# Batch one of an attention-and-mixer kernel read two steps per partition in all three pairs of chunks

## The chip, the core and the metric

The kernel runs on one core of a Trainium2 chip. A core has five engines with a queue of instructions each: TensorE (PE; weight loads, which overlap products, are shown apart as PEld), VectorE (DVE), ScalarE (ACT), GpSimd (POOL) and SyncE (SP), which here only issues DMAs. Sixteen DMA engines move the data. The metric is device time in microseconds (us), lower is better. Before the change it was 164.72 us, the median of 3 runs (164.44 to 165.76).

## The reference

The first half is a linear attention with a decaying state, for 4 batches, 8 heads, 768 steps and 48 values per head; the second half is an MLP mixer over its output (768 steps by 384 columns per batch).

```
for t in range(S):                                       # S = 768
    cur = einsum('bhd,bhe->bhde', u[None] * k[:, :, t], v[:, :, t])
    y[:, :, t] = einsum('bhd,bhde->bhe', r[:, :, t], state + cur)
    state = w[None, :, :, None] * state + einsum('bhd,bhe->bhde', k[:, :, t], v[:, :, t])

xt = x.transpose(0, 2, 1)                                # x: batch, 768, 384
h = maximum(xt @ w_tok1, 0) @ w_tok2                     # 768 -> 256 -> 768
u = x + h.transpose(0, 2, 1)
out = u + maximum(u @ w_ch1, 0) @ w_ch2                  # 384 -> 1536 -> 384
```

## The kernel before

**Attention in chunks.** Each batch's 768 steps are cut into six chunks of 128. For a chunk, k and r are multiplied by powers of the decay (tables `wnat`, `wp`, `wpair`; the products are called `kr`), turned on PE or by a DMA transpose, and multiplied with each other (`at_ps`); DVE masks the result to the earlier steps (`AT`). y is AT by v plus r by the state before the chunk (`S`). The state is kept in one bank for two or three chunks (`kv_ps`). The term of a step with itself goes apart: u-weighted sums of r by k (`pr`, `ad_ps`, `adg`), times v (`yd`, `ydb`), are added to y. The result of a chunk is `x_b`.

**Three ways of reading.** The list `STYLES` has one entry per chunk. "dma" (batches three and four): k, r and v of a chunk are loaded with one step per partition, so each piece of a load is 48 numbers, 192 bytes, and the turning is done by DMA. "f32" (chunks three to six of batch one, all of batch two): k and v as before, but r of a pair of chunks is loaded with two consecutive steps per partition, in pieces of 384 bytes (`window`, tile `win`); PE turns. "win" (the first pair of batch one): k, r and v are all loaded so, into one buffer of the pool `zr`, which later holds the mixer's hidden values; `pair_unit` computes the pair. In it each of the two halves j (even and odd steps) of a partition's row is scaled, turned and scored for itself, and the two chunks z of the pair lie in the upper and lower 64 partitions. So a product over one chunk's steps runs on 64 rows, twice, in place of once on 128.

**The mixer** of a batch follows: hidden products over steps (`h_ps<-x_b,wtok`, tasks `hid`), the transposed way back (`hx_ps`, `hT_ps`), up products (`z_ps<-uT,wch`), relu into `zr`, down products (`h_ps<-wch,zr`), output sums (`osb`) and stores. PE works on the up and down products of one batch while the others prepare the attention of the next.

**The order.** All work is entered as tasks; `ORDER` is a list of task numbers that says in which order they are written, and with that the order on every engine's queue. `BUFS` gives the buffer of each pool for each use, `ENGINES` the choice where a task can run on either of two engines, and `POOLS` the number of buffers. Nothing is reordered when the kernel runs: an engine whose next instruction waits holds up all behind it, and SP's queue so holds loads, DMA transposes and stores in one row. Sixteen tasks of products on a zero tile (`warm`) stand in PE's first 13 us. `GROUPS` says which chunks are scored together, `H1_PARTS` in which pieces the hidden products run, `PE_ADDS` for which chunks PE adds the own term.

**Names in the profile.** A line of nearly all rows is 279, that of the helper which records instructions, so rows are told apart by tiles. In `pair_unit` the turned k is `tk_ps` and its copy `ka`, the turned r `tr_ps` and its copy `rkb`; outside it they are `trk`, `rka`.

## Time and profile before

| | before |
|---|---|
| median of 3 runs | 164.72 us |
| the profiled execution | 164.68 us |
| its span, first to last instruction | 163.0 us |
| busy of the span: PE, DVE, ACT, POOL | 95%, 74%, 43%, 46% |
| moved by DMA | 26.90 MB in 90982 packets, 85714 of them under 512 B |
| first up product of batch one (z) | 32.9 us |
| last of PE's products ends | 159.4 us |

The profile is of one execution. The page gives busy time, the span in 40 slices of 4.07 us with a digit for tenths of a slice, the chain of waits that ended last, and groups of instructions. Other views give the instructions of an engine in order of time, busy time by stretches, and what one tile's instructions wait for. In rows of the order in time, the first number is the start and the second how long the group took, both in us; the brackets at the end name what the engine waited for ahead of it. Ends of products on PE are modelled, so the time that a group takes is best read from its start to the start of the next.

### The profile page before, as it was taken

Reading aid. Unit: us, or ns where it says so; the run is one execution under the profiler, and the core shown is the slowest. Engines: PE = TensorE matmul, PEld = TensorE weight load, DVE = VectorE, ACT = ScalarE, POOL = GpSimd, SP = SyncE. Lnnn points to the kernel's source line nnn. Section 1 sums busy time; section 2 is a strip of 40 time slices with the busy share of each in tenths; the row PEclk is TensorE's granted clock in tenths of the full one; section 3 lists DMA queues with packets and bytes.
Section 4 is the critical chain, followed back from the end, with each engine's and each line's share of the span. In section 5 each row is a group of like instructions: output and inputs, shape, how many; then the busy total and the mean of one; then the engine's idle time right before and its main releaser. Section 6 shows DMA issues by size and latency. Waiting matters only on the chain.

```text
span 163.0 us, 3866 instructions
## 1 busy us (share of the span) xinstructions
PE 154.6 (95%) x1513; PEld 104.6 (64%) x1513; DVE 120.2 (74%) x238; ACT 70.4 (43%) x162; POOL 75.2 (46%) x97
## 2 busy tenths in 40 slices
PE   6999399999999999899999999999999999999991
PEld 2457267677676768566666776777667666666670
DVE  6629997645699979998979989899598257741522
ACT  3948376586862577335262523056532101410400
POOL 7366657276007169798917947745824000000000
PEclk9999959999999999999999999999999999999999
DMA  4999999999996989999998997999971052530142
GB/s 124 262 220 190 210 211 206 196 216 192 218 200 134 191 152 182 194 195 201 189 179 172 223 221 131 201 245 180 196 189 49 2 117 67 136 120 0 48 147 99
DMA packets 90982, 26.90 MB, mean 165 GB/s; under 512 B 85714, under 2 KB 90068, under 8 KB 90964
## 3 DMA queue, kind: packets, MB, share of 16 engines
q1 hardware_dynamic: 88608, 23.40, 72.8%
q0 software_dynamic: 2160, 3.15, 11.4%
q8 instruction: 12, 0.20, 0.5%
q10 hardware_dynamic: 196, 0.11, 0.2%
q14 instruction: 6, 0.05, 0.1%
HBM read 20.46 MB, written 4.72 MB: 154 GB/s over the span
## 4 chain that ended last, share of the span: by engine, by line
PE 81%; DVE 8%; POOL 4%; issue 2%; DMA 2%; ACT 0%; DVEq 0%; ACTq 0%
PE z_ps L279 29%; PE h_ps L279 28%; PE y_ps L279 5%; PE kv_ps L279 5%; PE at_ps L279 3%; PE hT_ps L279 3%; PE hx_ps L279 2%; DVE kr L279 2%; POOL yd L279 2%; DMA out_dram<-osb 2%; DVE AT L279 2%; PE tr_ps L279 1%; PE trk L279 1%; DVE osb L279 1%; PE w_ps L279 1%
## 5 line engine op out<-in xcount | busy, mean ns | idle before, releaser
L279 PE MATMUL h_ps<-wch,zr 128*128 128x384 bf16 (+1 forms) x300 | 54.2, 320 | 0.0
L279 PE MATMUL z_ps<-uT,wch 128*128 128x384 bf16 x288 | 51.5, 326 | 0.0
L279 ACT ACTIVATE zr<-z_ps 128x384 bf16<-128x384 f32 x60 | 27.5, 490 | 45.0 <-PE z_ps L279 44.9
L279 PEld LDWEIGHTS <-wch 128*128 128x128 bf16 x288 | 31.6, 114 | 13.2
L279 PEld LDWEIGHTS <-zr 128*128 128x128 bf16 x300 | 27.5, 98 | 15.4
L279 DVE TENSOR_TENSOR AT<-at_ps,mask 128x512 bf16<-128x512 f32 x44 | 28.3, 683 | 1.2 <-PE at_ps L279 1.0
L279 DVE TENSOR_SCALAR zr<-z_ps 128x384 bf16<-128x384 f32 x36 | 19.2, 552 | 12.7 <-PE z_ps L279 12.4
L279 POOL TENSOR_TENSOR kr<-kt,wnat 128x384 bf16<-128x384 f32 x16 | 16.5, 1038 | 4.9 <-DMA kt<-in_k_dram 4.1
L279 POOL TENSOR_TENSOR yd<-vb,adg 128x384 f32<-128x384 bf16 x16 | 13.8, 866 | 6.3 <-DVE adg L279 6.1
L279 PEld LDWEIGHTS <-kr 128*128 128x128 bf16 (+1 forms) x184 | 12.0, 101 | 5.9 <-issue 2.1
L279 DVE TENSOR_TENSOR osb<-u_sb,h_ps 128x384 f32<-128x384 bf16 (+1 forms) x16 | 8.1, 524 | 6.3 <-PE h_ps L279 3.7
L279 POOL TENSOR_TENSOR ku<-kt,u_bc 128x384 f32<-128x384 f32 x10 | 9.9, 999 | 3.1 <-DMA kt<-in_k_dram 3.1
L279 DVE TENSOR_TENSOR x_b<-y_ps,yd 128x384 bf16<-128x384 f32 x18 | 9.5, 552 | 2.5 <-PE y_ps L279 1.6
L279 POOL TENSOR_TENSOR pr<-rka,rkb 128x512 bf16<-128x512 bf16 x3 | 3.6, 1210 | 15.3 <-DVE rkb L279 9.9
L279 ACT CAST vb<-vt 128x384 bf16<-128x384 f32 x19 | 9.6, 514 | 2.1 <-POOL yd L279 1.0
L279 PEld LDWEIGHTS <-wtok 128*128 128x128 bf16 x78 | 7.4, 98 | 4.6 <-issue 0.2
L279 DVE TENSOR_TENSOR u_sb<-x_b,hT_ps 128x384 bf16<-128x384 bf16 x15 | 7.7, 549 | 2.8 <-PE hT_ps L279 2.6
L279 ACT CAST S<-kv_ps 48x192 bf16<-48x192 f32 x24 | 7.5, 311 | 5.1 <-PE kv_ps L279 4.6
L279 POOL TENSOR_TENSOR rku<-ku,rt 128x384 f32<-128x384 f32 x7 | 7.2, 1031 | 4.3 <-DVE ku L279 4.2
L279 PE MATMUL y_ps<-vb,AT 128*128 128x48 bf16 (+1 forms) x208 | 8.9, 184 | 0.0
L279 PE MATMUL h_ps<-x_b,wtok 128*128 128x384 bf16 x48 | 8.8, 326 | 0.0
L279 PE MATMUL kv_ps<-warm 128*128 128x512 bf16 (+1 forms) x25 | 6.7, 425 | 1.3 <-DVE warm L279 1.3
(108 smaller groups left out, 201.6 us busy)
## 6 DMA issues: line engine op xcount, KB each, us to landing
out_dram<-osb SPq DMA_DIRECT2D x23, 192.0 KB, 2.3
kt<-in_k_dram SPq DMA_DIRECT2D x22, 192.0 KB, 5.3
vt<-in_v_dram SPq DMA_DIRECT2D x22, 192.0 KB, 4.3
rt<-in_r_dram SPq DMA_DIRECT2D x12, 192.0 KB, 3.6
win<-in_r_dram SPq DMA_DIRECT2D x5, 384.0 KB, 6.1
wch<-in_moe_w_ch_dram POOLq DMA_DIRECT2D x4, 384.0 KB, 6.7
wtok<-in_moe_w_tok_dram POOLq DMA_DIRECT2D x2, 384.0 KB, 6.2
wch<-in_moe_w_ch_dram POOLq DMA_DIRECT2D x1, 768.0 KB, 11.3
```

What stands on the lines that cost most here:

```text
L279: return lambda *args, **kw: tc.keep_in_program_order(f(*args, **kw))
```

## The change

All three pairs of batch one are now computed by `pair_unit`: `STYLES` has six "win" entries in place of two. The three rooms for their loads are three buffers of `zr`. The decay tables of k (`wk`), which lay in one of those buffers, go into two buffers of `u_sb`, and the two masks for pairs (`mask`, now bf16, and `spots`) share a third; `u_sb` is otherwise first wanted by a later half batch. The pools `ka`, `adg2` and `vb2` get a second buffer, `ydb` has three in place of four, `ku` two in place of three. `ORDER`, `BUFS` and `ENGINES` are new from end to end. The core of the diff, with a line or two of each table:

```diff
 ORDER = [
-    0, 3, 24, 54, 56, 1, 11, 895, 47, 55, 4, 2, 9, 900, 23, 6, 16, 59, 8, 13, 22, 888, 40, 7, 19, 25, 17, 12,
+    0, 3, 21, 18, 16, 56, 60, 13, 17, 59, 2, 879, 8, 5, 20, 57, 62, 872, 14, 6, 1, 42, 4, 27, 7, 11, 23, 9,
...
     'ydb': [
-    0, 1, 2, 3, 0, 1,
+    0, 1, 2, 0, 1, 0,
...
-GROUPS = [[(0, 1), (2,), (3,), (4,), (5,)], [(0, 1), (2, 3), (4, 5)], [(0, 1), (2, 3), (4, 5)],
+GROUPS = [[(0, 1), (2, 3), (4, 5)], [(0, 1), (2, 3), (4, 5)], [(0, 1), (2, 3), (4, 5)],
  [(0, 1), (2, 3), (4, 5)]]
-STYLES = 2 * [('win', 'pe')] + 10 * [('f32', 'pe')] + 12 * [('dma', 'dve')]
+STYLES = 6 * [('win', 'pe')] + 6 * [('f32', 'pe')] + 12 * [('dma', 'dve')]
...
-H1_PARTS = [[(0, 1, 2), (3, 4), (5,)], [(0, 1, 2, 3, 4, 5)], [(0, 1, 2, 3, 4, 5)], [(0, 1, 2, 3, 4, 5)]]
+H1_PARTS = [[(0, 1), (2, 3), (4, 5)], [(0, 1, 2, 3, 4, 5)], [(0, 1, 2, 3, 4, 5)], [(0, 1, 2, 3, 4, 5)]]
...
-POOLS = {'win': 3, 'ka': 1, 'rkb': 2, 'pr2': 1, 'adg2': 1, 'vb2': 1, 'ydb': 4, 'AT0': 3, 'AT1': 3}
+POOLS = {'win': 3, 'ka': 2, 'rkb': 2, 'pr2': 1, 'adg2': 2, 'vb2': 2, 'ydb': 3, 'AT0': 3, 'AT1': 3, 'ku': 2}
...
-    def early_room():
-        t = sb("zr", [128, 3, dm * 2], f32)
-        early["wk"] = t[:, 0, :].rearrange("p (j d) -> p j d", j=2)
-        early["mask"] = t[:, 1, 0:2 * T].rearrange("p (j t) -> p j t", j=2)
+    def early_wk(j):
+        def f():
+            early["wk", j] = sb("u_sb", [128, 3 * dm // 2], f32)[:, 0:dm]
+        return f
+
+    def early_masks():
+        t = sb("u_sb", [128, 3 * dm], bf16)
+        early["mask"], early["spots"] = (t[:, i * 2 * T:(i + 1) * 2 * T].rearrange("p (j t) -> p j t", j=2) for i in range(2))
...
     def two_steps(b, c, i):
-        return STYLE[b * C + c][0] == "win" or i == 1 and wide(b)
+        return STYLE[b * C][0] == "win" or i == 1 and wide(b)
...
     for b in range(B):
-        for c in range(0, C, 2):
-            if STYLE[b * C + c][0] == "win":
+        if STYLE[b * C][0] == "win":
+            for c in range(0, C, 2):
                 rooms[b, c] = room(b, c)
...
-            if STYLE[b * C + cs[0]][0] == "win":
+            if STYLE[b * C][0] == "win":
                 pair_unit(b, cs[0] // 2)
```

How this moves instructions shows on three engines. First DVE, from the copy of the first pair's turned k (`ka`) on; `AT` are the masks, `pr` the products of r and k, `S` a state, `win`, `kt` and `zr` the loads. Before:

```order
L279 COPY ka<-tk_ps 128x1024
L279 MEMSET S_1_95 128x192
L279 MEMSET S_0_94 128x192
L279 TENSOR_TENSOR pr_259<-tr_ps,ka 128x1024
L279 TENSOR_TENSOR AT_282<-at_ps,zr 128x512
L279 TENSOR_TENSOR AT_297<-at_ps,zr 128x512
L279 TENSOR_TENSOR AT_313<-at_ps,zr 128x512
L279 TENSOR_TENSOR AT_330<-at_ps,zr 128x512
L279 TENSOR_TENSOR kr_72<-win,wpair 128x8x48
L279 TENSOR_TENSOR kr_67<-kt,wnat_82 128x8x48
L279 TENSOR_TENSOR kr_72<-win,wpair 128x8x48
L279 TENSOR_TENSOR pr<-trk,rkb 128x512
```

With the change:

```order
L279 COPY ka<-tk_ps 128x1024
L279 TENSOR_TENSOR pr_252<-tr_ps,ka 128x1024
L279 TENSOR_TENSOR kr_71<-zr,u_sb 128x8x48
L279 TENSOR_TENSOR AT_310<-at_ps,u_sb 128x512
L279 TENSOR_TENSOR pr_324<-tr_ps,ka 128x1024
L279 TENSOR_TENSOR AT_331<-at_ps,u_sb 128x512
L279 TENSOR_TENSOR AT_364<-at_ps,u_sb 128x512
L279 TENSOR_TENSOR AT_377<-at_ps,u_sb 128x512
L279 TENSOR_TENSOR AT_409<-at_ps,u_sb 128x512
L279 TENSOR_TENSOR S_454<-kv_ps,wGm_91 128x384
L279 TENSOR_TENSOR AT_469<-at_ps,u_sb 128x512
L279 TENSOR_TENSOR pr_481<-tr_ps,ka 128x1024
```

The three scale products behind the first four masks are gone from this place; most of the second and third pairs' scale products now stand ahead of the copy of `ka`, and the masks of the pairs follow each other with the pairs' `pr` between them.

SP's first loads, in pieces of 96 numbers (two steps) or 48 (one). Before:

```order
L279 DMA zr<-in_r_dram 128x8x96
L279 DMA zr<-in_k_dram 128x8x96
L279 DMA win<-in_r_dram 128x8x96
L279 DMA zr<-in_v_dram 128x8x96
L279 DMA kt<-in_k_dram 128x8x48 x2
L279 DMA win<-in_r_dram 128x8x96
L279 DMA kt<-in_k_dram 128x8x48
L279 DMA vt<-in_v_dram 128x8x48
```

With the change:

```order
L279 DMA zr<-in_r_dram 128x8x96
L279 DMA zr<-in_k_dram 128x8x96 x2
L279 DMA zr<-in_r_dram 128x8x96
L279 DMA zr<-in_v_dram 128x8x96
L279 DMA zr<-in_k_dram 128x8x96
L279 DMA zr<-in_r_dram 128x8x96
L279 DMA zr<-in_v_dram 128x8x96
L279 DMA win<-in_r_dram 128x8x96
L279 DMA zr<-in_v_dram 128x8x96
```

Eight loads of k and v of 192 KB became four of 384 KB, the third pair's v stands tenth, and r of batch two (`win`) ahead of it.

POOL's queue from the first mixer weights (`wtok`) to the up weights (`wch`); `ydb` are the own terms. Before:

```order
L279 DMA wtok_98<-in_moe_w_tok_dram 128x6x256
L279 TENSOR_TENSOR ydb<-vb_234,adg_389 128x384 x2
L279 TENSOR_TENSOR kr_69<-kt,wnat_82 128x8x48
L279 TENSOR_TENSOR ydb<-vb,adg 128x384 x2
L279 DMA wtok_99<-in_moe_w_tok_dram 128x1536
L279 DMA wch_0_100<-in_moe_w_ch_dram 128x3x512
L279 DMA wch_1_101<-in_moe_w_ch_dram 128x3x1024
L279 TENSOR_TENSOR ydb<-vb,adg 128x384 x2
```

With the change:

```order
L279 DMA wtok_97<-in_moe_w_tok_dram 128x6x256
L279 TENSOR_TENSOR kr_71<-zr,u_sb 128x8x48
L279 TENSOR_TENSOR kr_72<-zr,wpair 128x8x48 x2
L279 TENSOR_TENSOR ydb<-vb_240,adg_333 128x384 x2
L279 TENSOR_TENSOR ydb<-vb_389,adg_387 128x384 x2
L279 TENSOR_TENSOR kr_67<-win,wpair 128x8x48
L279 DMA wtok_98<-in_moe_w_tok_dram 128x1536
L279 TENSOR_TENSOR ydb<-vb_560,adg_526 128x384 x2
L279 DMA wch_0_99<-in_moe_w_ch_dram 128x3x512
L279 DMA wch_1_100<-in_moe_w_ch_dram 128x3x1024
```

The second mixer weights now stand ahead of the last own terms, and the up weights behind them; three scale products more are POOL's.

## The prediction

> **What bounds the kernel now.** I read the page's slices first, then busy time stage by stage, then the order in time of TensorE (PE) and VectorE (DVE) in the first 33 us. The page:

> ```profile
> PE 154.6 (95%) x1513; PEld 104.6 (64%) x1513; DVE 120.2 (74%) x238; ACT 70.4 (43%) x162; POOL 75.2 (46%) x97
> ...
> PE   6999399999999999899999999999999999999991
> ```

> PE is busy 95% of the span; its one hole is the fifth slice (16.3 to 20.4 us). By stage (the columns are the stretch, its length, then busy us of PE, weight loads, DVE, ACT, POOL, then granted clock, DMA share, GB/s):

> ```profile
> 17.60:21.00 3.40, 1.53 (x23) 1.22 (x23) 3.40 (x6) 1.13 (x2) 1.35 (x2) 1.00 1.30 233
> 21.00:24.40 3.40, 3.40 (x44) 2.19 (x41) 3.29 (x8) 2.62 (x8) 2.38 (x4) 0.50 1.02 203
> 24.40:32.90 8.50, 8.47 (x116) 6.13 (x115) 5.88 (x12) 5.11 (x13) 3.90 (x5) 1.00 1.14 202
> 32.90:72.00 39.10, 38.48 (x419) 27.33 (x418) 31.92 (x59) 23.32 (x57) 21.34 (x23) 1.00 0.99 186
> 72.00:120.00 48.00, 48.00 (x453) 32.81 (x450) 42.45 (x83) 20.07 (x48) 32.60 (x35) 1.00 1.06 197
> 120.00:152.70 32.70, 32.70 (x257) 21.53 (x255) 18.17 (x37) 6.03 (x14) 2.48 (x3) 1.00 0.26 76
> ```

> From 32.9 us on PE idles 0.62 us until 152.7. So only two things can move the time: the moment at which the first z product starts (32.90), and new waits behind it. Between 17.6 and 21.0 PE works 1.53 us while DVE is full, and between 21.0 and 24.4 PE is full at half clock: that hole costs 1.87 us of waiting and about 1.7 us of clock. PE in order of time (start, us, what):

> ```profile
> 4.23 0.61 PE L279 MATMUL kv_ps<-warm 128*128 128x128 bf16 x4
> ...
> 5.39 1.62 PE L279 MATMUL u_ps<-wp,ones 1*128 1x384 f32 x2
> 6.95 2.74 PE L279 MATMUL kv_ps<-warm 128*128 128x512 bf16 x9
> 9.48 1.06 PE L279 MATMUL tr_ps<-ident,kr 128*128 128x128 bf16 x8
> ...
> 11.18 0.62 PE L279 MATMUL tk_ps<-ident,kr 128*128 128x128 bf16 x8
> 11.63 1.24 PE L279 MATMUL kv_ps<-warm 128*128 128x512 bf16 x5
> 12.81 0.64 PE L279 MATMUL at_ps<-rkb,ka 48*64 48x128 bf16 x32
> 13.38 0.51 PE L279 MATMUL kv_ps<-vb,kr 64*128 64x96 bf16 x8
> 13.82 0.62 PE L279 MATMUL tr_ps<-ident,kr 128*128 128x128 bf16 x8
> ...
> 15.74 0.74 PE L279 MATMUL y_ps<-vb,AT 64*128 64x48 bf16 x32
> 16.32 0.39 PE L279 MATMUL at_ps<-rkb,rka 48*128 48x128 bf16 x8
> ...
> 21.00 0.82 PE L279 MATMUL y_ps<-ydb,spots 64*128 64x384 bf16 x4
> 21.75 0.27 PE L279 MATMUL ad_ps<-u_blk,pr 128*128 128x8 bf16 x4
> ...
> 32.90 0.65 PE L279 MATMUL z_ps<-uT,wch 128*128 128x384 bf16 x3
> ```

> and DVE:

> ```profile
> 5.50 1.06 DVE L279 TENSOR_TENSOR kr<-zr,wpair 128x384 bf16<-128x384 f32 x2 [1.68 <-ACT wpair L279]
> ...
> 11.83 0.69 DVE L279 COPY ka<-tk_ps 128x1024 bf16<-128x1024 bf16 x1 [0.19 <-PE tk_ps L279]
> ...
> 12.86 0.63 DVE L279 TENSOR_TENSOR pr<-tr_ps,ka 128x1024 bf16<-128x1024 bf16 x1
> 13.40 2.47 DVE L279 TENSOR_TENSOR AT<-at_ps,zr 128x512 bf16<-128x512 f32 x4
> ...
> 18.03 1.34 DVE L279 TENSOR_TENSOR kr<-win,wpair 128x384 bf16<-128x384 f32 x1
> ...
> 25.53 1.88 DVE L279 TENSOR_TENSOR AT<-at_ps,mask 128x512 bf16<-128x512 f32 x3
> ```

> DVE's last mask product (AT) of batch one ends at 27.41; the first z follows 5.5 us later.

> **Step 1, the warm-up.** The first scale products wait for ACT's decay table (5.50), as they still will. The transposes behind them were ready far before 9.48: PE was still in its warm-up products, which took 2.53 us from 6.95 for six tasks of 512 columns, 0.42 us each. The broadcast of u (5.39 to 6.95) leaves this place and goes behind the first states; three more warm tasks come into it. From w's broadcast (which ends at 4.23) to the transposes now stand eleven tasks and two tiny products: 11 x 0.42 + 0.7 = 5.3, so 9.6 at the slow pace. If the unbroken row of products brings full pace (five in 1.17 us from 11.63) sooner, near 7.4, it is 8.7. I take 9.2; sixteen transposes take 0.9 (0.45 for eight, 13.38 to 13.82 for as many short ones) to 1.5 us, so both tiles stand at 10.4 in place of 11.8.

> [...]

> **Step 2, DVE up to the last mask.** Ahead of the copy of ka DVE now has seven scale products, u's product and two small ones: 7 x 0.53 + 0.8 = 4.5, so 10.0 without a wait. Beside a POOL product one of them took 1.34 us in place of 0.55, and the fourth load lands late, so I put ka at 10.9 (10.4 to 11.9). From there to the last mask stand ka 0.68, three products pr at 0.6, twelve masks at 0.62 (four in 2.47), two states at 0.5, one scale product at 0.55 to 1.34, one small copy: 0.7 + 1.8 + 7.4 + 1.0 + 0.9 + 0.2 = 12.0, so 22.9. Before, the same stretch took 15.6 us (11.83 to 27.41): the masks are twelve in both, but three scale products of over 1.1 us and four separate pr leave.

> **Step 3, PE in that stretch.** Two steps per partition need 80 more products in batch one. Chunks read one step per partition take, in the chain of work:

> ```profile
> 42.88 0.55 PE at_ps L279 x16
> ...
> 45.79 0.17 PE kv_ps L279 x4
> ```

> Per pair at full clock: scores 0.57 (12.81 to 13.38) against 0.55, states 2 x 0.44 (13.38 to 13.82) against 2 x 0.17, masks by v 0.58 (15.74 to 16.32) for 32 against some 0.4 for half as many, and the own term 0.75 at half clock (21.00 to 21.75), so 0.38 at full, against two products of 384 columns, 0.32. Two pairs, with three states between them, add 1.3 us (1.0 to 2.0). Summed over the new order from the first scores to the last y: scores 1.7, states 2.5, own 0.75, y 2.0, transposes 0.9, sums 0.6, u's broadcast 0.75, first mixer products 0.65: 9.9 us. From 11.6 that ends at 21.5, ahead of DVE's 22.9, so DVE sets the end and PE is full about 85% of the time, against 45% in the old hole; no half-clock window should follow. Waits that neither sum holds (POOL's scale products for pair three, its two own products per pair, the third v load) I put at 1.0 (0 to 2): the last mask ends at **23.9**, 3.5 us earlier.

> The 32 products of 48 columns took 18 ns each (0.58 us), the eight of 96 columns 55 ns (0.44 us): the price of a product here is no constant. [...]

> **Step 4, from the last mask to z.** In the new order PE has there:

> ```profile
> 28.90 0.65 PE h_ps L279 x4
> ...
> 30.21 0.45 PE tr_ps L279 x8
> 30.65 2.41 PE hx_ps L279 x18
> ```

> y 0.58, transposes 0.45, own 0.38, eight hidden products 1.3, the 30 of hx 3.1 (the 2.41 of 18 and twelve turns at 0.056, as the eight in 0.45), two k transposes 0.45, a state 0.17: 6.4 us. The copies of x and relu lie under k transposes and hx. z starts at **30.3**, 2.6 us earlier, and the k transposes and the state (0.6) are done ahead of it, which before followed it. Gain 3.2 us.

> At nothing I cost: the decay tables and masks in u's buffers (POOL and ACT write them while the first loads fly; batch two's second half wants those buffers first, near 70), the three rooms for loads (the first room is read out by 12, z wants it at 30), ACT's natural tables, which go from 7 to 13 us to behind the third v casts (ACT has 5.11 busy of the 8.50 us up to 32.9; without that room it would be 0.6 a table), and the last 10 us, which keep their order.

> **Step 5, loads.** Eight loads of k and v of batch one come as 384 B pieces, four of twice the size.

> ```profile
> 4.00:8.00 4.00, 3.87 (x15) 1.97 (x15) 2.50 (x6) 3.57 (x9) 1.45 (x5) 1.00 1.27 263
> 12.00:16.00 4.00, 4.00 (x89) 2.87 (x87) 4.00 (x9) 3.56 (x9) 2.41 (x4) 1.00 1.41 193
> ```

> The first stretch carried nearly only 384 B pieces, the second 192 B: 393 KB in 1.50 us against 2.04, so 2.2 us less DMA time. Ten such loads ahead of and with the third pair's v are 15 us from about 2 on, with the first weights between some 17: it lands near 19, and its states stand on PE at about 20.5 by the sum of step 3. POOL's queue has wch behind the third pair's own products, whose second buffer comes free only after pair two's own term on PE (near 21.7): issue near 23. Before:

> ```profile
> 24.18 1.51 POOL L279 DMA_DIRECT2D wch<-in_moe_w_ch_dram  x2
> ...
> DMA to landing us min/median/max: 5.3/6.8/11.3
> ```

> The long one landed near 36.2 and was wanted 24 z products and two short pieces after the first z (24 x 0.163 + 0.4 = 4.3 us, so 37.2); now about 35 against 34.6. I add 0.5 us for this and for what follows in batches three and four (0 to 3).

> **Sum.** The profiled execution took 164.68, its span 163.0 and 1.7 around it; the median of the runs is 164.72, so nothing is lost between them. 163.0 - 2.6 - 0.6 + 0.5 = 160.3, with 1.7 around it **162.0 us**.

> **Rivals.** *The loads become the pace.* DMA is at a share of 1.06 from 72 to 120 us, and the new order wants batch four's x some 4 us earlier, of which the larger pieces free 2.2; the stretch from 32.9 to 72, at 0.99, leaves little more. If the rest isn't found in gaps of the queue, PE waits about 1.5 us there: 163.5. For it speaks the share, against it that PE never waited for a load behind 21 us. *A low-activity window again*, where DVE lags PE between 14 and 23: 1.7 us lost at half clock, 163.7; the sum of 85% speaks against it. *A fixed price per product:* 80 at the dearer row's 55 ns are 4.4 in place of 1.3 in step 3, 165.1; the row of 18 ns leaves it a chance of 0.02. [...] *Slower: the last v load behind two stores.*

> ```profile
> 117.84 0.38 SPq L279 DMA_DIRECT2D vt<-in_v_dram  x1
> ...
> L279 ACT CAST vb<-vt x5: 502/512/512, 92.0 to 123.7; 128x384 bf16<-128x384 f32 x5
> ...
> DMA to landing us min/median/max: 3.3/3.6/3.9
> ```

> The last v load of batch four went out at 117.84, could land at 121.4 and was cast at 123.7: 2.3 us of slack. In the new queue two stores stand right ahead of it, and they wait for output sums, which wait for PE's down products. With y 3.2 us earlier it must go out by 116.9; each us later is a us for PE, and from 121.3 on the kernel is over 1% slower. At 122 it gives about 167. For it: the queue's own order. Against it: PE has eight down products ahead of the scores there.

> **How the numbers follow.** A measurement of this kernel can tell about 1% (1.6 us) from no change. Forecast kept (159.5 to 163.0): 0.58. The gain is eaten by loads 0.12, by a half-clock window 0.08, by price per product or several small waits 0.05: together 0.25 within 1%. Slower by over 1%: 0.17, most of it the store rival, as the whole order of four batches is new and only its first fifth was summed here. Low end: DVE without a wait (1.0), no later wait (0.5), the 0.62 us wait of the second batch gone, warm-up at full pace (0.5): 159.3. High end: 166.0, which leaves about 0.13 above and 0.06 below.

> **What would show it.** First transposes near 9.2; last mask of batch one near 23.9; first z near 30.3; clock 1.00 from 11 us on; products of 64 rows at the same times; no PE wait over 1 us behind z. Wrong if z starts after 32, if PE waits for wch near 34.5, or if a row of PE waits for vb, rk or h1r near 110 to 122.

## The result and the profile after

| | before | with the change |
|---|---|---|
| median of 20 runs each | 165.12 us (164.15 to 166.37) | 163.91 us (161.72 to 166.28) |
| ratio to before | | 0.990, 95% interval 0.987 to 0.993 |
| the profiled execution, its span | 164.68 us, 163.0 us | 165.22 us, 163.3 us |
| first z of batch one | 32.90 us | 34.79 us |
| from there to the end of the span | 130.1 us | 128.5 us |

The change gains about 1%, where 162.0 us was forecast. The time lies above the 159.5 to 163.0 of "forecast kept", in the part of the range in which the gain is eaten (a chance of 0.25 by the prediction), and the gain is less than half of what was forecast. Ratios here and below leave out runs that stand out as slow, most of those at the lowest clock among them; medians are of all runs. The profiled execution is one of the slower ones. From its page, the lines on PE and its clock:

```profile
PE 158.4 (97%) x1593; PEld 106.9 (65%) x1593; DVE 119.5 (73%) x239; ACT 66.2 (41%) x149; POOL 79.6 (49%) x101
...
PE   6999999999999999999999999999999999999991
...
PEclk9998555999999999999999999999999999999999
```

The hole in PE's fifth slice is gone, as planned. But PE's clock is at half for more than three slices in which PE is full. The stretches (length, then busy us of PE, weight loads, DVE, ACT, POOL, granted clock, DMA share, GB/s), cut where the clock changes, once in between (at 11.48), and where z starts:

```profile
8.06:11.48 3.42, 3.42 (x46) 2.82 (x45) 3.10 (x9) 2.25 (x6) 2.19 (x3) 1.00 1.28 261
11.48:14.89 3.41, 3.11 (x79) 2.03 (x77) 2.94 (x6) 3.16 (x8) 3.25 (x4) 1.00 1.27 261
14.89:28.54 13.65, 13.65 (x212) 9.60 (x214) 9.36 (x17) 7.78 (x16) 8.60 (x11) 0.50 1.07 208
28.54:34.79 6.25, 6.25 (x94) 4.51 (x89) 3.83 (x8) 3.28 (x7) 3.49 (x6) 1.00 1.13 192
34.79:72.00 37.21, 37.21 (x402) 26.39 (x400) 30.96 (x63) 16.52 (x40) 20.93 (x22) 1.00 0.98 187
72.00:120.00 48.00, 48.00 (x464) 32.41 (x462) 41.46 (x76) 22.29 (x52) 36.25 (x38) 1.00 1.07 195
```

Half clock lasts 13.65 us, four times 3.41, and PE works through all of it; in the 3.41 us ahead PE was busy 3.11. Before, one such stretch of 3.40 us followed 1.53 us of work. DVE, which was to be the pace, has 9.36 busy of 13.65. Of the 20 runs seven had a mean clock of 1.00 (spans 159.8 to 162.1 us), four 0.975 to 0.977 (161.6 to 162.0) and nine 0.954 to 0.958 (163.2 to 164.4). The median spans of the three groups are 161.6, 161.95 and 163.3 us. So the lowest clock costs 1.7 us in the median, the middle one 0.35, and the seven runs at 1.00 still spread over 2.3 us; their median time, 163.37 us, is 1.4 us over the forecast. Experiments 7 and 8 bear on that part.

### The profile page after: what moved, and what is told of

It is laid out like the page before. It is cut to its first block, busy times and chain, and to the rows that moved or that the text cites. A ratio compares the mean times of both kernels' runs of the same rounds, so it can differ in the third digit from the quotient of the medians.

```text
span 163.3 us, 4001 instructions
## 1 busy us (share of the span) xinstructions
PE 158.4 (97%) x1593; PEld 106.9 (65%) x1593; DVE 119.5 (73%) x239; ACT 66.2 (41%) x149; POOL 79.6 (49%) x101
## 4 chain that ended last, share of the span: by engine, by line
PE 94%; ACT 2%; DVE 1%; issue 0%
PE h_ps L279 35%; PE z_ps L279 29%; PE kv_ps L279 8%; PE y_ps L279 7%; PE at_ps L279 4%; PE hT_ps L279 3%; PE hx_ps L279 3%; PE tr_ps L279 2%; ACT rkb L279 1%; PE w_ps L279 1%; PE trk L279 1%; PE ad_ps L279 1%; PE tk_ps L279 1%; ACT ka L279 1%; ACT vb L279 1%; DVE pr L279 0%
## 5 line engine op out<-in xcount | busy, mean ns | idle before, releaser
L279 PE MATMUL h_ps<-wch,zr 128*128 128x384 bf16 (+1 forms) x300 | 54.0, 319 | 0.0
L279 PE MATMUL z_ps<-uT,wch 128*128 128x384 bf16 x288 | 52.3, 327 | 0.0
L279 ACT ACTIVATE zr<-z_ps 128x384 bf16<-128x384 f32 x61 | 28.1, 491 | 51.6 <-PE z_ps L279 51.5
L279 PEld LDWEIGHTS <-wch 128*128 128x128 bf16 x288 | 31.7, 114 | 13.5
L279 PEld LDWEIGHTS <-zr 128*128 128x128 bf16 x300 | 27.4, 97 | 15.2
L279 DVE TENSOR_SCALAR zr<-z_ps 128x384 bf16<-128x384 f32 x35 | 18.4, 554 | 14.0 <-PE z_ps L279 13.9
L279 DVE TENSOR_TENSOR AT<-at_ps,mask 128x512 bf16<-128x512 f32 x36 | 23.2, 681 | 3.2 <-PE at_ps L279 3.2
L279 POOL TENSOR_TENSOR yd<-vb,adg 128x384 f32<-128x384 bf16 x13 | 10.7, 830 | 17.8 <-ACT vb L279 5.1
L279 PEld LDWEIGHTS <-kr 128*128 128x128 bf16 (+1 forms) x196 | 13.3, 107 | 3.5 <-issue 1.1
L279 POOL TENSOR_TENSOR kr<-kt,wnat 128x384 bf16<-128x384 f32 x13 | 13.3, 1026 | 1.7 <-DMA kt<-in_k_dram 0.9
L279 POOL TENSOR_TENSOR ku<-kt,u_bc 128x384 f32<-128x384 f32 x11 | 12.0, 1088 | 2.3 <-DMA kt<-in_k_dram 1.6
L279 DVE TENSOR_TENSOR osb<-u_sb,h_ps 128x384 f32<-128x384 bf16 (+1 forms) x16 | 8.4, 525 | 4.9 <-PE h_ps L279 4.8
L279 PEld LDWEIGHTS <-wtok 128*128 128x128 bf16 x78 | 7.3, 100 | 5.2 <-issue 1.3
L279 DVE TENSOR_TENSOR x_b<-y_ps,yd 128x384 bf16<-128x384 f32 x18 | 9.6, 552 | 1.4 <-PE y_ps L279 1.2
L279 DVE TENSOR_TENSOR u_sb<-x_b,hT_ps 128x384 bf16<-128x384 bf16 x15 | 7.5, 549 | 4.0 <-PE hT_ps L279 4.0
L279 PE MATMUL h_ps<-x_b,wtok 128*128 128x384 bf16 x48 | 9.4, 342 | 0.0
L279 POOL TENSOR_TENSOR rku<-ku,rt 128x384 f32<-128x384 f32 x8 | 8.6, 1079 | 1.3 <-DMA rt<-in_r_dram 1.1
L279 POOL TENSOR_TENSOR pr<-rka,rkb 128x512 bf16<-128x512 bf16 x3 | 3.6, 1213 | 11.5 <-DVE rka L279 4.6
L279 PE MATMUL kv_ps<-vb,kr 128*128 128x96 bf16 (+1 forms) x100 | 8.8, 228 | 0.0
L279 PE MATMUL y_ps<-vb,AT 128*128 128x48 bf16 (+1 forms) x240 | 8.8, 191 | 0.0
L279 POOL TENSOR_TENSOR kr<-rt,wp 128x384 bf16<-128x384 f32 x8 | 8.6, 1081 | 0.0
L279 ACT CAST S<-kv_ps 48x192 bf16<-48x192 f32 x20 | 6.3, 313 | 5.2 <-PE kv_ps L279 5.0
```

Of the source, the lines that this page charges most:

```text
L279: return lambda *args, **kw: tc.keep_in_program_order(f(*args, **kw))
```

## The experiments

**1. The change again, and the kernel before again** (no edit).

> The changed kernel unchanged, for a profile with another clock. In the profile at hand PE is full from 14.9 to 28.5 us but the granted clock is 0.5 there, and z starts at 34.79. If the low clock (theory A) is all that separates it from the forecast, a run whose clock never falls starts z near 30.5 and spans about 160; if DVE, POOL or the loads set the pace there anyway (theory B), z starts at 32 to 33.5 with full clock and the span is 161 to 162. Behind z both expect 128.5 us, as in the profile at hand.

> The kernel before, for its spread and its clock in each run: one low window of 3.4 us (mean clock 0.99) in most runs, spans of 162.5 to 164.5. Where a run shows no low window, theory A says that it is 1.0 to 1.7 us shorter; theory B says the same as the others within 0.5 us.

The change took 161.89 us, span 160.1, and its clock stayed at 1.00 from 6.80 us on, with z at 30.79: what theory A expected (30.5 and 160). It is a look at the forecast at full clock, in one of the fastest runs of this kernel. Its stretches, with the columns as above:

```profile
6.80:10.21 3.41, 3.41 (x40) 2.68 (x39) 3.21 (x10) 1.55 (x4) 1.09 (x1) 1.00 1.28 261
10.21:13.63 3.42, 3.19 (x67) 2.16 (x63) 2.84 (x5) 3.12 (x7) 3.26 (x5) 1.00 1.27 261
13.63:17.04 3.41, 3.06 (x98) 2.53 (x98) 3.41 (x7) 2.70 (x6) 3.41 (x5) 1.00 1.35 234
17.04:20.45 3.41, 2.92 (x72) 2.08 (x70) 3.01 (x6) 2.01 (x4) 2.43 (x4) 1.00 1.28 247
20.45:30.79 10.34, 9.70 (x160) 6.66 (x157) 8.77 (x17) 7.22 (x16) 6.18 (x10) 1.00 1.06 189
```

The four longest of PE's waits over the whole span (us in total, times, longest):

```profile
PE kv_ps L279 <- DVE warm L279: 1.3, 1, 1.3
PE ad_ps L279 <- DVE pr L279: 0.6, 2, 0.3
PE z_ps L279 <- DVE AT L279: 0.5, 1, 0.5
PE z_ps L279 <- DMA wch<-in_moe_w_ch_dram: 0.3, 1, 0.3
```

PE idles 0.23 to 0.49 us in each of three windows, 1.07 us in all, where the half-clock run had 0.30 ahead of the fall, and the clock stays up. PE's order in time:

```profile
8.49 0.61 PE L279 MATMUL tr_ps<-ident,kr 128*128 128x128 bf16 x8
...
11.04 0.42 PE L279 MATMUL at_ps<-rkb,ka 48*64 48x128 bf16 x16
...
12.76 0.91 PE L279 MATMUL u_ps<-wp,ones 1*128 1x384 f32 x2
...
23.93 0.57 PE L279 MATMUL y_ps<-vb,AT 64*128 64x48 bf16 x32
...
30.79 0.68 PE L279 MATMUL z_ps<-uT,wch 128*128 128x384 bf16 x3 [0.32 <-DMA wch<-in_moe_w_ch_dram]
...
35.49 5.53 PE L279 MATMUL z_ps<-uT,wch 128*128 128x384 bf16 x33
```

And DVE's, the copy of `ka` and the last masks of batch one:

```profile
10.14 0.69 DVE L279 COPY ka<-tk_ps 128x1024 bf16<-128x1024 bf16 x1
...
20.94 1.88 DVE L279 TENSOR_TENSOR AT<-at_ps,u_sb 128x512 bf16<-128x512 f32 x3
```

The same places in the profile at half clock:

```profile
11.55 0.42 PE L279 MATMUL at_ps<-rkb,ka 48*64 48x128 bf16 x16
11.90 0.35 PE L279 MATMUL ad_ps<-u_blk,pr 128*128 128x8 bf16 x8
12.19 0.42 PE L279 MATMUL at_ps<-rkb,ka 48*64 48x128 bf16 x16
12.54 0.51 PE L279 MATMUL kv_ps<-vb,kr 64*128 64x96 bf16 x8
12.98 0.91 PE L279 MATMUL u_ps<-wp,ones 1*128 1x384 f32 x2
14.18 0.36 PE L279 MATMUL ad_ps<-u_blk,pr 128*128 128x8 bf16 x8 [0.30 <-DVE pr L279]
14.47 0.42 PE L279 MATMUL at_ps<-rkb,ka 48*64 48x128 bf16 x16
...
34.79 0.65 PE L279 MATMUL z_ps<-uT,wch 128*128 128x384 bf16 x3
```

From first scores to first z: 19.75 us at full clock, 23.24 at half. Between these two runs the low clock costs 3.5 us up to z, of which 0.8 comes back behind it (129.3 against 128.5 us to the end). The kernel before gave 165.37 us (ratio 1.005, interval 0.998 to 1.012), with half clock for 6.83 us: its own hole costs it one or two windows in each run (mean clock 0.975 to 0.990 in all ten). Three runs with one window (0.989 to 0.990) span 161.9 to 162.9 us, the seven with more 163.2 to 164.7.

**2. Blocks of products behind the kernel.**

```diff
     plan.run()
...
+        full(80)
+        for i in range(200):
+            pe.matmul(b[:, 0:96], wtok1[half(0), 0, 0:128], x_bs[1][half(0), 0, 0:96], ...)
+        full(80)
+        for i in range(70):
+            pe.matmul(b[:, 0:384], wtok1[half(0), 0, 0:128], x_bs[1][half(0), 0, :], ...)
+        full(80)
+        for i in range(500):
+            z = i % 2
+            pe.matmul(b2[z][:, 0:48], wtok1[half(z), 0, 0:128], x_bs[1][half(z), 0, 0:48], ...)
+        full(80)
+        for i in range(500):
+            q, z = i % 2, i // 2 % 2
+            rows = slice(q * P, q * P + D)
+            pe.matmul(b2[q][half(z), 0:128], wtok1[rows, 0, 0:64], x_bs[1][rows, 0, 0:128], ...)
+        full(80)
```

> The changed kernel with rows of products behind its last store, about 10 us each, divided by full products of 128 rows and 384 columns: 128 rows by 96 columns; 64 rows by 96; 64 rows by 384; 64 rows by 48 alternating between both halves of the rows; 48 rows by 64 weight columns by 128, alternating. Nothing waits in them. Theory A1 (the clock's monitor counts how much of the array works, so products of half the rows pull the clock down): clock 1.00 in the rows of 128, 0.50 in at least the 64 x 96 and 64 x 384 rows after 3.4 to 6.8 us. Theory A2 (the clock falls for gaps between products, as waits make them): 1.00 in all. Theory A3 (short products, whatever their rows, pull it down): 0.50 in 128 x 96 too, 1.00 in 64 x 384.

`full(n)` are n products of 384 columns on the whole array. The 200 products of 64 rows and 96 columns and the 70 of 384 ran at clock 1.00 for 20 us: half rows by themselves did not bring the clock down. The 500 short ones did, those on quarters did not:

```profile
246.16:249.57 3.41, 1.73 (x139) 1.62 (x132) 0.00 (x0) 0.00 (x0) 0.00 (x0) 1.00 0.02 5
249.57:252.98 3.41, 2.48 (x128) 2.35 (x122) 0.00 (x0) 0.00 (x0) 0.00 (x0) 0.50 0.02 5
273.46:276.88 3.42, 1.95 (x142) 1.79 (x135) 0.00 (x0) 0.00 (x0) 0.00 (x0) 1.00 0.02 5
```

The first window was followed by half clock with PE busy 1.73, the last was not with 1.95; in both PE also stood for over 1 us (1.68 and 1.47) in which it waited for nothing that the profile shows. So the theory of half rows falls in the form in which it was put. Gaps and short products are left, and so is a count by the part of the array in use, which puts both of these windows at the edge (shares of 0.37 each).

**3. One filling product of 128 rows ahead of each group of half-row products.**

```diff
-FILL = {}
+FILL = {144: 1, 141: 1, 170: 1, 173: 1, 199: 1, 202: 1, 147: 1, 149: 1, 176: 1, 178: 1, 205: 1, 151: 1, 180: 1, 207: 1}
```

> The changed kernel with one full product on the zero tile (128 rows, 384 or 512 columns) ahead of each of 14 groups of half-row products in batch one: the six of scores, five of states, three of y; about 2.7 us more work for PE at full clock. Theory A1: the share of full products in each window rises by some 20%, the clock falls in fewer runs or not at all, spans 161 to 162.5 and none near 163.3. Theory A2: clock as without (0.954 to 1.0 by run), spans 1 to 3 us longer than without.

`FILL` puts products of the zero tile ahead of a task's own: here the six score groups, five states and three y. Median 164.05 us, ratio 0.986 (0.981 to 0.991); eight of ten runs at a clock of 0.997 or more. PE has more work, and the clock stays up more often than in the 20 runs without (seven at 1.00). Against the expectation, two runs at 0.979 were left, and five had spans of 162.9 to 164.0, three of these at full clock.

**4. Rows or columns?**

```diff
     plan.run()
...
+        def block(rows, cols, n):
+            for i in range(n):
+                pe.matmul(b[0:cols, 0:384], wtok1[0:rows, 0, 0:cols], x_bs[1][0:rows, 0, :], ...)
...
+        block(128, 64, 100)
+        full(70)
+        block(64, 64, 100)
...
+        for i in range(16):
+            pe.matmul(b[:, 0:384], ones[0:1, 0:128], u_bc[0:1, 0:384], start=True, stop=True, skip_group_check=True)
```

> The changed kernel with a tail of products that wait for nothing, each block some 16 us (some five clock windows of 3.41 us) of 384 columns, between blocks of 70 products on the whole array (11 us, full clock). Blocks in order, with the part of the 128 x 128 array that a product uses: 100 products of 128 rows x 64 columns (0.50), 100 of 64 x 64 (0.25), 100 of 112 x 64 (0.44), 100 of 96 x 64 (0.375), 100 of 80 x 64 (0.31), then 16 fp32 products of one row (under 0.01). Theory 'used array' (the clock falls to half behind a window in which products, each weighted by the part of the array that it uses, fill less than about 0.37 of the window; worked out from the earlier profiles, where windows at 0.23 to 0.37 were followed by half clock and windows at 0.38 to 0.83 were not): clock 1.00 through the 0.50 and 0.44 blocks, 0.50 from the second window on in the 0.25 and 0.31 blocks and in the one-row block, the 0.375 block on the edge. Rival 'gaps' (only time without a product counts): 1.00 in every block, since nothing waits in them. Rival 'short products': 1.00 in every block, since each has 384 columns. Time about 320 us if no block falls, some 15 to 25 us more if three of them run most of their length at half clock.

```profile
168.70:184.70 16.00, 16.00 (x100) 10.59 (x99) 0.00 (x0) 0.00 (x0) 0.00 (x0) 1.00 0.00 1
...
196.00:212.00 16.00, 16.00 (x100) 10.38 (x98) 0.00 (x0) 0.00 (x0) 0.00 (x0) 1.00 0.00 1
...
304.50:325.00 20.50, 20.50 (x51) 10.49 (x49) 0.00 (x0) 0.00 (x0) 0.00 (x0) 0.64 0.00 1
```

"Used array" was wrong for the blocks on half the columns: all five, the 64 x 64 one too, kept 1.00 (340.0 us in all). Only in the one-row block did the clock fall, from 310.4 to 327.5 us, with PE busy throughout and 384 columns in each product, which neither gaps nor short products allow. These one-row products are fp32 and the other blocks bf16; the next experiment has them in bf16. So rows count here (16.00 us at 1.00 with 64 of them, half clock with one) and columns don't (64 of 128 kept 1.00); to fit the windows of the kernel as well, two products side by side on the halves of the columns have to count once.

**5. The same fourteen products, one row high.**

```diff
-            pe.matmul(bank, warm[:, 0:128], warm[:, 0:bank.shape[-1]], start=fresh, stop=True, skip_group_check=True)
+            pe.matmul(bank, warm[0:1, 0:128], warm[0:1, 0:bank.shape[-1]], start=fresh, stop=True, skip_group_check=True)
```

> The run with fourteen filling products, each now of one row in place of 128: the same number, places, columns and length, so TensorE is as busy, but they use under 0.01 of the array. Theory 'used array': they no longer hold the clock up and they thin the windows out, so nearly every run has one or more windows at half clock (mean clock 0.94 to 0.98), the first z near 37, time 165.5 to 168. Rivals 'gaps' and 'short products': the same clock and time as with products of 128 rows (median 164.05, clock 0.997 or more in eight of ten runs).

```profile
13.14:16.55 3.41, 3.41 (x66) 2.37 (x65) 2.27 (x5) 2.21 (x4) 3.08 (x5) 1.00 1.33 243
16.55:40.45 23.90, 23.90 (x285) 12.96 (x284) 10.27 (x19) 9.13 (x22) 10.04 (x14) 0.50 1.04 188
```

173.69 us, ratio 1.037 (1.033 to 1.042), all four runs at 0.931 to 0.940. With number, place, type and columns of the products kept, the rows alone decide: PE is busy in every moment of 27.3 us and at half clock for 23.9 of them. The sign was forecast, the size not (165.5 to 168): once down, the clock stayed down for seven windows.

**6. u's broadcast moved ahead of the first z.**

```diff
 ORDER = [
-    147, 162, 163, 51, 71, 188, 143, 136, 148, 164, 170, 145, 186, 52, 189, 142, 149, 165, 166, 173, 171, 151,
+    147, 162, 163, 71, 188, 143, 136, 148, 164, 170, 145, 186, 189, 142, 149, 165, 166, 173, 171, 151, 167,
...
-    336, 226, 232, 221, 76, 229, 227, 234, 233, 326, 235, 240, 230, 327, 236, 241, 258, 328, 347, 259, 264,
+    226, 232, 221, 76, 229, 227, 51, 234, 233, 326, 235, 52, 240, 230, 327, 236, 241, 258, 328, 347, 259, 264,
```

> The changed kernel with the broadcast of u (two fp32 products of one row, 0.91 us of TensorE at under 0.01 of the array) moved from between the first states to just ahead of batch one's first z product, its copy behind it; nothing else. Theory 'used array': the windows from 10 to 18 us, at 0.23 to 0.38 before, rise by about 0.1, so the clock stays full in most runs (before: 9 of 20 runs at a mean of 0.954 to 0.958), and the runs that were at 163.2 to 164.4 us of span join the others at 160 to 162; median 162.5 to 163.3, ratio to the kernel before 0.975 to 0.985. Rivals: the share of low runs stays at about half, since TensorE waits for VectorE as often as before, or more with 0.9 us of work gone ahead of it; median 163.9, ratio 0.99.

The expectation failed: the median is 165.28 us in place of 162.5 to 163.3, with three of six runs at 0.959. PE in its order:

```profile
12.23 0.51 PE L279 MATMUL kv_ps<-vb,kr 64*128 64x96 bf16 x8
13.93 0.36 PE L279 MATMUL ad_ps<-u_blk,pr 128*128 128x8 bf16 x8 [1.19 <-DVE pr L279]
```

PE came sooner to its wait for VectorE's `pr` and stood 1.19 us; a wait adds as little to the share as one-row products (0.32 in the window from 10.64, and 0.32 in the window of the same start in `clock_bench`, where u is in its place).

**7. Filling products where the share is lowest, beside the change itself.** In the full-clock run of 1 the share of a window of 3.41 us that starts at 11.0 would be 0.18 (two score groups and the start of a third, one state, u's one-row products), from 13.5 on over 0.40. `fill_early` keeps u's place, `fill_gap` is built on the kernel of 6.

```diff
-FILL = {}
+FILL = {144: 1, 141: 1, 147: 2, 170: 1, 149: 1, 173: 1}
```

and for `fill_gap`:

```diff
-FILL = {}
+FILL = {141: 1, 147: 4, 170: 1, 173: 1}
```

> The changed kernel once more, beside the two kernels with filling products on the same chip. Theory 'used rows' (the clock falls to half behind a window of 3.41 us in which products, each weighted by its rows out of 128 and by half where two of them run side by side on the two halves of the columns, fill less than 0.37; so far 26 windows at 0.01 to 0.37 were followed by half clock and every window at 0.37 or more by full clock): a window that starts between 10.3 and 13.2 us is at 0.18 to 0.34, one that starts earlier or later is above 0.37, so about 3 of 3.41 starting points lead into half clock except where the neighbour's share is close; 40 to 70% of the runs show a mean clock under 0.98, at spans 1 to 3 us longer than the others. Ratio to the kernel before 0.985 to 0.995.

> The changed kernel with seven filling products of 128 rows, all ahead of the third pair: one ahead of each of the first two score groups, two ahead of the first state, one ahead of the next state and of each of the second pair's scores (1.3 us of TensorE, of which 0.5 to 0.9 lies in its waits for VectorE). Theory 'used rows': the poorest window rises from 0.18 to about 0.40, so nearly all runs stay at full clock (0.99 or more); batch one's first z comes 0.3 to 0.6 us later than in a full-clock run without them; spans 160.5 to 162.5, median time 162.5 to 163.5, ratio 0.975 to 0.987. Rival (only waiting time counts, or chance): as many low runs as in the kernel without them, time 0.5 us over it.

> The kernel with u's broadcast moved ahead of the first z, with seven filling products of 128 rows: four ahead of the first state, in the 1.19 us in which TensorE waited there, one ahead of three of the score groups (1.3 us of TensorE). Theory 'used rows': the poorest window rises from 0.18 to about 0.43; nearly all runs at a clock of 0.99 or more where three of six were at 0.959 without them; spans 160.5 to 162.5, median time 162.5 to 163.5, ratio 0.975 to 0.987. Rival: half the runs stay at 0.959 and 166.6 us.

| | median, lowest to highest, us | ratio to before | runs at a clock of 0.99 or more |
|---|---|---|---|
| the change itself | 164.48 (161.93 to 165.85) | 0.986 (0.981 to 0.991) | 3 of 6 |
| `fill_early` | 163.42 (162.45 to 165.81) | 0.989 (0.985 to 0.993) | 7 of 8 |
| `fill_gap` | 163.59 (162.40 to 164.89) | 0.989 (0.984 to 0.994) | 6 of 6 |

The ratios look alike; the last column tells the kernels apart: 13 of 14 runs with filling products keep the clock, and 10 of 26 of the change in its two series. The medians differ by about 1 us, in ranges that overlap. The one low run of `fill_early` is its profiled one: its window from 12.08 had a share of 0.368 where 0.40 was meant, and half clock followed. The clock behind the first scores is settled, but spans at full clock still run from 160.5 to 163.1. Where the clock first rises differs between profiles: between 6.6 and 8.7 us in six of ten, with the first scores at 11.0 to 12.1; between 12.1 and 13.3 in the other four, with the scores at 13.6 to 14.2. `fill_gap` is one of the four:

```profile
7.33 0.59 PE L279 MATMUL wd_ps<-ident_f,wp 8*128 8x8 f32 x2
7.85 0.61 PE L279 MATMUL kv_ps<-warm 128*128 128x512 bf16 x1
8.39 0.59 PE L279 MATMUL ud_ps<-ident_f,wp 8*128 8x8 f32 x2
...
9.73 1.06 PE L279 MATMUL tr_ps<-ident,kr 128*128 128x128 bf16 x8
```

Ahead of the first rise products run at half pace: the eight transposes above took 1.06 us, those in the run of 1 (8.49, at full clock) 0.61. So even full products reach a share of only 0.5 there, and two tiny pairs of products, 1.2 us together, take a window that starts near 6 to 0.32. The views print a clock of 1.00 for the time ahead of the first rise as well (0.00 to 8.06 us in the first profile of the change), so a mean clock of 1.00 doesn't tell when it came.

**8. u's tiny products taken out of the warm-up,** in both kernels of 7.

```diff
 ORDER = [
-    131, 34, 883, 126, 884, 66, 127, 29, 155, 876, 30, 48, 64, 156, 40, 880, 871, 159, 132, 50, 69, 128, 160,
-    133, 46, 873, 885, 129, 157, 43, 137, 67, 161, 134, 138, 119, 886, 144, 184, 158, 135, 73, 141, 146, 185,
+    131, 34, 883, 126, 884, 66, 127, 29, 155, 876, 30, 64, 156, 40, 880, 871, 159, 132, 69, 128, 160, 133, 46,
+    873, 885, 129, 48, 157, 43, 50, 137, 67, 161, 134, 138, 119, 886, 144, 184, 158, 135, 73, 141, 146, 185,
```

> The kernel with u's broadcast ahead of the first z and seven filling products, and now the transposed u (two tiny fp32 products, 0.59 us at half clock, under 0.01 of the rows' work) taken out of the warm-up and put behind the second k transposes, its cast on VectorE behind the copy of ka. Theory 'used rows': at half clock a window can hold at most 0.50, so 0.9 us of such products in one window (0.5 x (1 - 0.9 / 3.41) = 0.37) keep the clock down; with w's and u's tiny products together in a window that starts between 5.3 and 7.5 us the first rise comes at 12.1 to 13.3 us and the first scores at 13.6 to 14.2 (four of ten profiles so far), otherwise at 6.6 to 8.7 us and 11.0 to 12.2. With only w's in it (0.5 x (1 - 0.6 / 3.41) = 0.41) the rise comes by 10.2 us in every run and the first scores by 12.7: the longest spans (162.3 to 163.1 in three of six runs) go to 161.5 or less; median time 162.3 to 163.0, lowest unchanged at 162.4, ratio to the kernel before 0.975 to 0.985. Rival (the warm-up ends when its loads and tables are there, whatever the clock): spans as before, 160.5 to 163.1, median 163.6.

> The same move of the tiny products of u in the other kernel with seven filling products (u's broadcast stays between the first states). Theory 'used rows': the first rise by 10.2 us in every run here too; the runs at 162.9 to 163.9 us of span (two of eight) go, unless a window that starts near 12 us falls below 0.37 (0.368 in the one profile that did); median time 162.3 to 163.2, ratio 0.975 to 0.987. Rival: spans stay at 160.7 to 163.9, median 163.4.

`ud_late` (on `fill_gap`): median **162.78 us** (162.23 to 163.22), ratio 0.983 (0.978 to 0.988), six of six runs at 1.00, spans 160.4 to 161.3. The forecast held, as far as one profile can show it: the clock rose at 8.97, the first scores started at 12.00:

```profile
10.46 0.38 PE L279 MATMUL ud_ps<-ident_f,wp 8*128 8x8 f32 x2
...
12.00 0.42 PE L279 MATMUL at_ps<-rkb,ka 48*64 48x128 bf16 x16
```

It is faster than the kernel before. Against the change, by the medians of all runs, it stands at 0.983 of the kernel before measured beside it, where the change stands at 0.993 and 0.996 in its two series; it is the lowest median here. `ud_early` had a median of 163.38 us, ratio 0.985 (0.979 to 0.990), five runs at 1.00 and spans of 160.2 to 161.9, and one of 199.95 us that no theory expected (last section).

## Why the prediction came out as it did

**The sum came out in one of the fastest runs, at full clock, and in part by luck.** The run of 1 had z at 30.79 (forecast 30.3), a span of 160.1 (160.3), 161.89 us (162.0). Step by step:

| | forecast | at full clock |
|---|---|---|
| first transposes (step 1) | 9.2 | 8.49 |
| copy of `ka` (step 2) | 10.9 | 10.14 |
| PE's work, first scores to last y (step 3) | 9.9 us | 12.1 us |
| last mask ends (steps 2, 3) | 23.9 | 22.82 |
| last mask to z (step 4) | 6.4 us | 7.97 us |
| z to the end (step 5) | 130.0 us | 129.3 us |

Step 2's length is as summed: from `ka` to the last mask 12.7 us against 12.0 and a wait of 1.0. Step 3's sum of PE was 2.2 us short (from 11.04 to 24.43 are 13.4 us, 1.3 of them waits): y took 2.7 in place of 2.0, states 2.9 in place of 2.5, and the rest lies in smaller pieces. So PE's last y products start 1.1 us behind the last mask, and this is most of the 1.6 us that step 4 lacks. An early start (0.8), a shorter step 2 (0.3) and 0.7 us less behind z made up for it. The 80 more products cost what the rows of 64-row products gave, and the rival of a fixed price each fell: 32 of them took 0.57 us, 18 ns each, in the new order too (23.93).

**The step that failed is the end of step 3:** "PE is full about 85% of the time", so "no half-clock window should follow". In the profiled execution z started at 34.79, behind the 32 that the prediction gave as a sign of being wrong. PE was busy 90% of the time in that stretch at full clock (9.17 of 10.24 us from 10.21 to 20.45) and 98% at half clock (16.76 of 17.06 from 11.48 to 28.54), so PE was as full as forecast, and the conclusion did not follow. What decided is the share of rows. One window of the profiled execution, worked out: from 11.48 to 14.89 stand 48 score products (`at_ps`; each 128 columns x 0.42 ns x 48/128 x 1/2 = 10 ns), eight state products (`kv_ps`; 20 ns each), 16 sums of 8 columns (`ad_ps`; 3 ns each) and u's products (`u_ps`; one row), together 0.7 us; with the last warm products that is 0.23 of the window. Half clock then made products take longer (eight transposes 1.04 us from 18.27, 0.62 from 28.92 at full clock), so a window held fewer of them: the same work, which at full clock holds a share of 0.43 to 0.46 (13.63 to 20.45 in the run of 1), came to 0.34 to 0.36 and did not lift the clock again. It rose only behind the window from 25.13, which holds hidden products of 128 rows (0.43). The change had put the half-row products of three pairs in one row and left the full ones to the end.

Over thirteen profiles (all but that of `ud_early`; up to 155 us, and to the end in the two with blocks behind the kernel) the share sorts the windows: 30 of them, at 0.01 to 0.368, were followed by half clock, and 609, at 0.366 and up, by full clock. Transposes on PE count in it like other products: without them the window of `fill_gap` from 9.55, behind which the clock rose, would have 0.16 in place of 0.50. The rule was fitted to the profiles of 1 to 6; what filling does in 7 and the warm-up in 8 was forecast by it. Its first form, by the part of the array in use, got the one-row products right and missed u's move and the blocks on half the columns. That products side by side count once rests on the fit alone. Which runs get a half-clock window is a matter of where the windows lie: from 10.21 and 10.04 the share was 0.38 and 0.40 and the clock stayed, from 10.64 and 11.48 it was 0.32 and 0.23 and it fell.

**A second part is the warm-up of step 1.** It reckoned with full pace by the first scores and put at most 0.9 us (8.7 against 9.6) between an early and a late rise of the clock. Its 7.4 us for the early rise was an estimate; six of the ten profiles up to `fill_gap` had 6.6 to 8.7. In the other four the rise came at 12.1 to 13.3 us and the first scores at 13.6 to 14.2 in place of 11.0 to 12.1; the two of these whose clock then stayed up, `after_fill1` and `fill_gap`, span 162.9 and 162.7 us, against 160.1 for the run of 1. With u's tiny products out of the warm-up, all six runs of `ud_late` spanned 160.4 to 161.3, where those of `fill_gap`, from which it differs in this move (and the buffers that go with it), went from 160.5 to 163.1. That it also lengthened the slower runs at 1.00 of the change itself is likely, but none of those was profiled.

**The rivals.** *A low-activity window again* was what happened, at a chance of 0.08 and a price of 1.7 us; it came in 13 of 20 runs. Its chance was taken from busy time, which was not what counted (23.9 us at half clock without an idle moment in 5). Its price was taken from a single window; four windows cost 1.7 us between the median spans of the groups of runs, and 3.2 us of span between the two profiles compared in 1. *The loads become the pace* fell: in the run of 1 PE's waits for DMA are 0.32 us, all for `wch` ahead of z (0.9 to 1.1 in three profiles with half-clock windows; step 5 had 0.5 for this), and none for batch four's loads. *The last v load behind two stores* fell too: from z to the end no profile of the change is longer (128.5 to 129.3 us) than before (130.1).

## What to carry to other kernels

Look at the granted clock beside the busy share, and sum rows times columns, not products: here a stretch of half-row products with one-row ones among them was full of work, and the clock fell to half and stayed there for 13.65 us (23.9 us with fourteen more one-row products). Mix whole-row products into such a stretch, in places where the engine waits anyway, and keep tiny products apart in the warm-up; here seven filling products and four moved tasks gave 1.1 to 1.7 us in the median, across series, and the spread was 1.0 us in six runs, where the change had 3.9 in six and 4.6 in twenty. A profile of one execution shows one position of the clock's windows (one from 11.48, at 0.23, in the first profile of the change, one from 10.21, at 0.38, in the run of 1): look at the clock of all runs before a gain is read from one.

## What was not expected of the hardware

One run of `ud_early` was at a clock of 0.75 from 6.84 us to its end, on one core and with nothing in its order that the other five runs lacked. Its page:

```profile
PE 192.8 (97%) x1599; PEld 120.8 (61%) x1600; DVE 123.7 (62%) x239; ACT 66.4 (34%) x149; POOL 80.6 (41%) x101
...
PEclk9877777777777777777777777777777777777777
...
L279 PE MATMUL h_ps<-wch,zr 128*128 128x384 bf16 (+1 forms) x300 | 68.7, 388 | 0.0
```

The down products took 388 ns in the mean where the profile of the change has 319. It didn't come again in the five other runs, and its cause is open. Also open is why spans at full clock still differ by 1 us in `ud_late`.
